# Moving the q and k transposes of an attention stage from TensorE to VectorE, with block-wise loads

## The chip, the core and the metric

The kernel runs on one core of one Trainium2 chip. The core has five instruction queues: TensorE (PE; its weight loads are listed as PEld), VectorE (DVE), ScalarE (ACT), GpSimd (POOL) and SyncE (SP), which here issues nearly all DMAs. They share SBUF; PE writes its results to PSUM. The metric is the device time of one execution in microseconds (us), lower is better.

## The reference, cut to what matters

A chain of three blocks: causal attention with a decay, then two MoE-like stacks of dense products. The change is in the attention.

```python
# q, k, v: (4, 8, 576, 64) float32;  f: (4, 8, 576)
scores = (1 / sqrt(64)) * q @ k.T
cum = cumsum(log(clip(f, 1e-4, 1)))
scores = where(causal, -1e9, scores + cum[:, None] - cum[None, :])
attn = exp(scores - max(scores)); attn = attn / (sum(attn) + 1e-9)
x = attn @ v            # heads side by side: (2304, 512)
h = (x @ w1) * (x @ w2) @ w3 @ w_out
h = h @ w_in            # 2048 wide
out = rational(h) @ w_out2
```

## The kernel before, in words

The order of all instructions is written out by hand; every engine runs its own queue in that order. The 32 heads are taken in 16 pairs, so that the two heads of 64 columns fill 128 partitions. A head has five steps (c = 0 to 4), one per chunk of 128 query rows (the last has 64), and step t = 5n + c of head n issues work of several heads: the scores of chunk c (`score_mm`, PE), their row-maximum (`score_max`, DVE, line 381), the exponential of the chunk before (`score_exp`, ACT, line 392), the normalisation of a group of chunks (`score_rcp` on DVE, `score_norm` on POOL, line 407), the transposes of the normalised probabilities of the next chunk in turn (`p_transpose`, PE, line 412) and their split in a high and a low part (`p_split`, ACT line 436 and DVE line 438; for heads below 8 a plain copy, lines 427 and 429). At the end of step 4 comes P x V of the head before (`pv`, PE into `ps_v`), for heads below 8 `pv_early` (PE into `ps_w`).

Every matrix product is done in three parts with operands split in a high and a low part. So q and k of a pair need d on the partitions, scaled and split. Before the change: `load_pair` (lines 286 to 292) brings rows of q or k into `q_raw` or `k_raw` with three DMAs, and `qk_transpose` (lines 301 to 304) transposes them on PE in five instructions into `v_ps`, 576 columns of the PSUM tile `ps_v` that `pv` also writes. `prep` (lines 306 to 315) then makes the high part on ACT (line 311, with the factor QKS = 1/8 for q) and the low part on DVE (line 313). `stack_q` and `stack_k` (lines 357 and 368) spread the parts over the operand tiles `qs`, `qb`, `kh`, `kc` with nine SBUF-to-SBUF DMAs, some of which wait for one another; `load_rows` (lines 330 and 331) adds the rows of `cum`. All these DMAs are issued by SP, in program order.

For pair p+1 this happens while pair p is worked on: at even n, q is transposed in step 1 (line 647) and prepared in step 2; k is transposed at the end of step 2 (line 715), after q's parts are read, and prepared in step 3. `load_rows` come in steps 0 and 1, the stack DMAs in steps 2 to 4. At odd n, the loads of pair p+2 are issued in steps 0 (q) and 1 (k), and those of v in step 4. The first pair is transposed ahead of the loop (lines 597 and 598), from other tiles for k.

Into these steps two further streams are woven: decoding of the weights (`HalfDecoder`: loads d_r on SP line 68, DVE lines 151 and 154, ACT, POOL), at steps listed in `DEC_AT` and later in steps 1 and 3; and, from head 9 on, filler matmuls: the products of the batch before with w1 and w2 (`gen_ab`, into the two banks `ps_f`, with a copy on ACT, line 550, and a product on DVE, line 553). `fill` issues them by a fixed credit per step. After the last head (about 370 us) come the remaining fillers and the dense stacks.

Of the kernel before, what the change touches and what calls it, by code (L numbers as in the profile page):

```python
# [19 lines left out]
P = 128  # L20
NCH = 5
# [12 lines left out]
def raw(ap):  # L34
    return ap.bitcast(F32)
# [138 lines left out]
def kernel(  # L174
# [78 lines left out]
    a_sb = [xp.tile([P, HB], F32, name=f"a_sb{i}") for i in range(2)]  # L253
    c_sb = [xp.tile([P, HB], F32, name=f"c_sb{i}") for i in range(3)]

    q_raw = ap_.tile([P, NCH, 2, D], F32, name="q_raw")
    k_raw = ap_.tile([P, NCH, 2, D], F32, name="k_raw")
    v_raw = ap_.tile([P, NCH, 2, D], F32, name="v_raw")
    vhl = [ap_.tile([P, NCH, 2, 2 * D], F32R, name=f"vhl{i}") for i in range(2)]

# [22 lines left out]
    def flat(t):  # L283
        return t.rearrange("p h d -> p (h d)")

    def load_pair(p, t, src):
        b, h0 = divmod(2 * p, H)
        for j in range(2):
            nc.sync.dma_start(
                t[:, 0:4, j], src[b, h0 + j, 0:512, :].rearrange("(c p) d -> p c d", p=P)  # L290
            )
        nc.sync.dma_start(t[0:64, 4], src[b, h0 : h0 + 2, 512:S, :].rearrange("h p d -> p h d"))
# [5 lines left out]
            out=t[:, :, :, D : 2 * D], in0=v_raw, in1=raw(t[:, :, :, 0:D]), op=ALU.subtract  # L298
        )

    def qk_transpose(t, ps, ps4):
        for c in range(4):
            nc.tensor.transpose(ps[:, P * c : P * (c + 1)], flat(t[:, c]), ident)  # L303
        nc.tensor.transpose(ps4, flat(t[0:64, 4]), ident[0:64, 0:64])

    def prep(p, w, step):
        i = p % 2
        h, l = (kh[i][0], klt) if w else (qs[i][0], qs[i][1])
        scale = 1.0 if w else QKS
        if step == 0:  # L310
            nc.scalar.mul(h, v_ps, scale)
        else:
            nc.vector.scalar_tensor_tensor(
                out=l, in0=v_ps, scalar=scale, in1=raw(h), op0=ALU.mult, op1=ALU.subtract
            )

    def rows_once(i):

# [13 lines left out]

    def first_q(j):
        r, o = HALF[j], HALF[1 - j]
        nc.scalar.mul(qs[0][j][r], v_ps[r], QKS)
        nc.vector.scalar_tensor_tensor(
            out=qs[0][j][o], in0=v_ps[r], scalar=QKS, in1=raw(qs[0][j][r]),
            op0=ALU.mult, op1=ALU.subtract,
        )
        nc.gpsimd.tensor_copy(qb[0][j][r], raw(qs[0][j][r]))  # L340

# [36 lines left out]
    def score_max(n, c, part):  # L378
        r, t = QN[c], NCH * n + c
        a, b = (0, min(EXT[c], 512)) if part == 0 else (512, EXT[c])  # L380
        nc.vector.tensor_tensor_reduce(  # L381
            out=pr[0:r, OFF[c] + a : OFF[c] + b],
            in0=ps_s[(t + part) % 2][0:r, 0 : b - a],
            in1=mask[0:r, 512 - Q0[c] + a : 512 - Q0[c] + b],
            scale=-1.0, scalar=3.0e38 if part == 0 else st4[0:r], op0=ALU.add, op1=ALU.min,
            accum_out=st4[0:r] if part == 0 and EXT[c] > 512 else st[0:r, 0, c : c + 1],
        )

# [183 lines left out]
    def fill(ns):  # L572
# [10 lines left out]
            credit[0] = 0.0  # L583

    nc.sync.dma_start(lf, f.rearrange("b h s -> (b h) s"))
    load_pair(0, q_raw, q)
    load_pair(0, k_raw, k)
    side.append(gen_w12())
    side_step()
    nc.gpsimd.memset(one, 1.0)  # L590
# [1 line left out]
    nc.vector.tensor_scalar(lf, lf, 1e-4, 1.0, op0=ALU.max, op1=ALU.min)  # L592
    nc.scalar.activation(lf, lf, AF.Ln)
    nc.vector.tensor_tensor_scan(cum, one, lf, 0.0, ALU.mult, ALU.add)
    nc.scalar.copy(crow[:, 0], cum)
    nc.vector.tensor_tensor(out=crow[:, 1], in0=cum, in1=raw(crow[:, 0]), op=ALU.subtract)
    qk_transpose(q_raw, v_ps, v_ps[:, 512:S])
    qk_transpose(k_raw, w_ps, w_ps[:, 512:S])
    first_q(0)
    first_k(0)  # L600
    load_pair(1, q_raw, q)
    load_rows(0, raw(crow[0:1]))
    load_rows(1, raw(crow[1:2]))
    load_pair(1, k_raw, k)
    nc.sync.dma_start(crow_dr, raw(crow))
    load_pair(0, vf[0], v)
    w12["dec"].ahead = 2
    nc.gpsimd.memset(mask, 0.0)
    nc.gpsimd.affine_select(
        mask[:, 512:], mask[:, 512:], pattern=[[-1, P]], compare_op=ALU.is_ge, fill=NEG, base=0,  # L610
        channel_multiplier=1,
    )
    nc.gpsimd.memset(st, 1.0)
# [10 lines left out]
    for t in range(NCH * (NH + 1) + 2):  # L624
        n, c = divmod(t, NCH)
        p, x = n // 2, t % 2
        live = n < NH
        m, cc = (n - 1, c + 1) if c < NCH - 1 else (n, 0)
        turn = 0 <= m < NH
        even = n % 2 == 0 and p + 1 < NPAIR  # L630
        if n < N32:
            grp = {3: (n, 0, 3), 0: (n - 1, 3, 5)}.get(c)
        else:
            grp = {2: (n, 0, 2), 4: (n, 2, 4), 0: (n - 1, 3 if n == N32 else 4, 5)}.get(c)
        if grp and not 0 <= grp[0] < NH:
            grp = None
        if turn:
            p_transpose(x, cc)
        if live and EXT[c] > 512:
            score_mm(n, c, 1)  # L640
        if live and c < NCH - 1:
            score_mm(n, c + 1, 0)
        if 0 <= n - 1 < N32:
            for qc in {2: (0, 1, 2), 3: (3,), 4: (4,)}.get(c, ()):
                pv_early(n - 1, qc)
        if even and c == 1:
            qk_transpose(q_raw, v_ps, v_ps[:, 512:S])
        if 0 < t <= NCH * NH:
            score_exp((c - 1) % NCH)
        if live:  # L650
            score_max(n, c, 0)
        if c == 1 and 0 <= n - 2 < N32:
            x_low(n - 2)
        if grp:
            score_rcp(grp[1], grp[2], 0)
        if late_x is not None:
            p_split(1 - x, *late_x, 1)
        if grp:
            score_rcp(grp[1], grp[2], 1)
        if live and EXT[c] > 512:  # L660
            score_max(n, c, 1)
        flush()
        if t == 10:
            w12["dec"].ahead = 4
        if t == T_X1:
            x_split(H + 1)
            side.append(gen_wo2())
            side_step()
            dec_due = False
        dec_now = t in DEC_AT or (t > T_X1 and c in (1, 3))  # L670
        if dec_now:
            side_step()
        if t == 0:
            first_q(1)
            first_k(1)
            rows_once(1)
            for tile_ in (v_raw, *vf):
                nc.gpsimd.memset(tile_[64:128, 4], 0.0)
            nc.gpsimd.memset(pr[0:64, OFF[4] + S : OFF[4] + 5 * P], 0.0)
            nc.sync.dma_start(pa_sb, pa.unsqueeze(0).to_broadcast([P, 4]))  # L680
            nc.sync.dma_start(pb_sb, pb.unsqueeze(0).to_broadcast([P, 2]))
        if even and c in (2, 3):
            prep(p + 1, c - 2, 0)
            prep(p + 1, c - 2, 1)
        if grp:
            for g in range(grp[1], grp[2]):
                score_norm(grp[0], g)
        if dec_due:
            side_step()
        dec_due = dec_now  # L690
        late_x = None
        if turn:
            p_split(x, m, cc, 0)
            late_x = (m, cc)
        if c == 0 and 0 <= n - 2 < NH:
            pv_out(n - 2)
        if c == 1 and n - 1 == N32:
            psw.close()
            psf = ps1.enter_context(
                tc.tile_pool(name="psf", bufs=1, space=PSUM, reuse_waits="tile")  # L700
            )
            ps_f += [psf.tile([P, 512], F32, name=f"ps_f{i}") for i in range(2)]
        if c == 1 and n % 2 == 1 and N32 <= n - 2 < NH and n not in (H + 3, H + 5, H + 7):
            x_split(n - 2)
        if n == H + 8 and c in (1, 3):
            x_split(H + 2 + c)
        if c == 4 and n % 2 == 0 and N32 <= n < NH:
            split_v(p)
        if c == 2 and n > H and n % H == 1 and n < NH:
            fillers.append(gen_ab(n // H - 1))  # L710
        if n == 4 and c == 2:
            nc.scalar.activation(pb_abs, pb_sb, AF.Abs)
        fill(FILL1[c])
        if even and c == 2:
            qk_transpose(k_raw, v_ps, v_ps[:, 512:S])
        if c == NCH - 1 and N32 <= n - 1 < NH:
            pv(n - 1)
        if c == NCH - 1 and n == N32:
            early.close()
            lp = late.enter_context(pool("late", "left"))  # L720
            pt += [lp.tile([P, NCH, PTS], F32R, name=f"pt{part}") for part in "hl"]
        if c == NCH - 1 and n + 1 < NH:
            score_mm(n + 1, 0, 0)
        if even and c < 2:
            load_rows(2 * (p + 1) + c)
        if even and c >= 2:
            stack_q(p + 1, c - 2)
        if even and c >= 3:
            stack_k(p + 1, c - 3)
        if n % 2 == 1 and p + 2 < NPAIR:  # L730
            if c == 0:
                load_pair(p + 2, q_raw, q)
            if c == 1:
                load_pair(p + 2, k_raw, k)
        if n % 2 == 1 and p + 1 < NPAIR:
            if c == 4:
                load_pair(p + 1, vf[(p + 1) % 2] if 2 * (p + 1) < N32 else v_raw, v)
# [333 lines left out]
```

## Time and profile before

| | |
|---|---|
| median of 3 runs | 1006.69 us (1006.63 to 1007.95) |
| the profiled execution: span from first to last instruction | 1007.3 us |
| busy time of DVE | 760.4 us (75%) |
| busy time of ACT | 658.0 us (65%) |
| busy time of POOL | 386.5 us (38%) |
| q1, the queue of all DMAs of SP: packets, share of 16 engines | 125808, 39.3% |

For the profiled execution no other time than its span is listed. Busy times of engines overlap and are averages over stages with different limits; a time in square brackets in a row is how long the engine stood idle before that instruction, and for what. Matmuls are pipelined, so the time from the start of one to the start of the next says more than the duration of one.

### The profile page before, as it was taken

What the parts mean: (1) busy time and instruction counts of PE and PEld (TensorE: products, weight loads), DVE (VectorE), ACT (ScalarE), POOL (GpSimd) and SP (SyncE); (2) the same over time, 40 slices, a digit from 0 to 9 for tenths busy, and PEclk for the clock granted to TensorE, in tenths of its full rate; (3) what the DMA queues carried; (4) which work ended last, traced back from release to release, by engine and by line L of the source; (5) the groups of instructions that cost most, each with busy time, mean ns of one, the idle gap of its engine ahead of it and who ended that gap; (6) DMA issues with size and microseconds to landing.
All of it is one profiled execution on the core that took longest, in us unless ns stands there. A gap on an engine that the chain in (4) does not pass through costs nothing.

```text
span 1007.3 us, 18126 instructions
## 1 busy us (share of the span) xinstructions
PE 978.1 (97%) x6032; PEld 859.5 (85%) x6032; DVE 760.4 (75%) x1690; ACT 658.0 (65%) x1443; POOL 386.5 (38%) x468
## 2 busy tenths in 40 slices
PE   6898999999999999999999999999999999999998
PEld 4676989999999999998899898888888888888886
DVE  5677886777777764979877729888788878877886
ACT  5677775766666663535555538767676767767686
POOL 7556772544444442644444302222222222222222
PEclk9999999999999999999999999999999999999999
DMA  5877664566666633664677651001001100100010
GB/s 130 216 179 199 187 141 116 145 186 182 175 175 183 165 103 111 199 211 160 201 246 242 211 159 37 1 14 70 1 1 42 43 1 8 37 20 1 1 43 21
DMA packets 125903, 114.94 MB, mean 114 GB/s; under 512 B 65521, under 2 KB 92145, under 8 KB 125809
## 3 DMA queue, kind: packets, MB, share of 16 engines
q1 hardware_dynamic: 125808, 113.79, 39.3%
q8 instruction: 47, 0.77, 0.3%
q14 instruction: 48, 0.39, 0.1%
HBM read 70.61 MB, written 23.22 MB: 93 GB/s over the span
## 4 chain that ended last, share of the span: by engine, by line
PE 79%; DVE 5%; DMA 3%; ACT 3%; issue 2%; SPq 1%; POOL 0%; ACTq 0%; DVEq 0%
PE bank L213 44%; PE ps_f L213 19%; PE ps_v L213 6%; PE ps_s L213 4%; PE ps_x L412 3%; PE ps_v L303 1%; DMA kh<-kh 1%; DMA wo2l<-wo_dr 1%; ACT rr L986 1%; DMA d_r<-in_moe_w_in_dram 1%; ACT rr L987 1%; DMA z_dr<-z_sb 1%; DVE pp L999 0%; DMA cl<-c_dr 0%; SPq L812 0%
## 5 line engine op out<-in xcount | busy, mean ns | idle before, releaser
L968 POOL TENSOR_TENSOR gl<-pp,gh 128x512 fp32r<-128x512 f32 (+1 forms) x80 | 95.3, 1191 | 318.5 <-ACT gh L967 312.0
L407 POOL TENSOR_SCALAR pr<-pr,st 128x128 f32<-128x128 f32 (+4 forms) x160 | 92.6, 590 | 145.2 <-DVE st L402 60.7
L381 DVE CUSTOM_DVE_ANT_0 pr<-ps_s,mask 128x128 f32<-128x128 f32 (+4 forms) x160 | 83.7, 523 | 71.4 <-PE ps_s L213 65.9
L213 PE MATMUL bank<-ch,wil 128*128 128x512 f32 (+1 forms) x320 | 118.3, 370 | 0.0
L213 PE MATMUL bank<-cl,wih 128*128 128x512 f32 (+1 forms) x320 | 118.2, 369 | 0.0
L213 PE MATMUL bank<-ch,wih 128*128 128x512 f32 (+1 forms) x320 | 117.8, 368 | 0.0
L213 PE MATMUL bank<-wo2h,gh 128*128 128x512 f32 x288 | 114.2, 397 | 0.8 <-ACT gh L967 0.8
L213 PE MATMUL bank<-wo2h,gl 128*128 128x512 f32 x288 | 114.1, 396 | 0.3
L213 PE MATMUL bank<-wo2l,gh 128*128 128x512 f32 x288 | 113.9, 396 | 0.0
L975 ACT ACTIVATE h<-bank 128x512 f32<-128x512 f32 (+1 forms) x80 | 44.3, 554 | 98.5 <-PE bank L213 98.4
L392 ACT ACTIVATE pr<-pr,st 128x128 f32<-128x128 f32 (+4 forms) x160 | 97.3, 608 | 12.7 <-DVE st L381 12.2
L982 DVE SCALAR_TENSOR_TENSOR qv<-h,pb_abs,qv 128x512 f32<-128x512 f32 (+1 forms) x80 | 55.8, 697 | 41.1 <-ACT qv L976 41.1
L436 ACT CAST pth<-ps_x 128x256 fp32r<-128x256 f32 (+1 forms) x96 | 44.5, 463 | 63.0 <-PE ps_x L412 43.5
L213 PE MATMUL bank<-cl,w3oh 128*128 128x256 f32 x288 | 81.4, 283 | 2.2 <-DVE cl L492 2.1
L213 PE MATMUL bank<-ch,w3oh 128*128 128x256 f32 x288 | 80.8, 280 | 1.1 <-ACT ch L491 1.0
L213 PE MATMUL bank<-ch,w3ol 128*128 128x256 f32 x288 | 80.6, 280 | 0.5 <-DVE w3ol L843 0.5
L412 PE MATMUL ps_x<-ident,pr 128*128 128x128 f32 (+1 forms) x480 | 74.7, 264 | 6.4 <-POOL pr L407 3.4
L213 PE MATMUL ps_s<-kh,qs 128*128 128x128 f32 (+2 forms) x192 | 75.6, 394 | 4.1 <-DMA kh<-kh 1.8
L992 DVE SCALAR_TENSOR_TENSOR qv<-qv,rr 128x512 f32<-128x512 f32 (+1 forms) x80 | 51.4, 643 | 28.5 <-ACT rr L987 28.5
L213 PEld LDWEIGHTS bank<-cl,wih 128*128 128x128 f32 x320 | 60.2, 188 | 11.7
L213 PEld LDWEIGHTS bank<-ch,wih 128*128 128x128 f32 x320 | 60.2, 188 | 11.7
L213 PEld LDWEIGHTS bank<-ch,wil 128*128 128x128 f32 x320 | 60.2, 188 | 10.3
(169 smaller groups left out, 3003.1 us busy)
## 6 DMA issues: line engine op xcount, KB each, us to landing
d_r<-in_moe_w_out_dram SPq DMA_DIRECT2D x48, 256.0 KB
c_dr<-c_sb SPq DMA_DIRECT2D x64, 144.0 KB
cl<-c_dr SPq DMA_DIRECT2D x36, 256.0 KB
d_r<-in_moe_w_dram SPq DMA_DIRECT2D x16, 512.0 KB
d_r<-in_moe_w_dram SPq DMA_DIRECT2D x32, 256.0 KB
d_r<-in_moe_w_in_dram SPq DMA_DIRECT2D x32, 256.0 KB
kh<-kh SPq DMA_DIRECT2D x45, 144.0 KB
z_dr<-z_sb SPq DMA_DIRECT2D x36, 128.0 KB
```

The costliest lines, as they stand in the source:

```text
L213: nc.tensor.matmul(o, lhsT, rhs, start=start, stop=stop)
L303: nc.tensor.transpose(ps[:, P * c : P * (c + 1)], flat(t[:, c]), ident)
L381: nc.vector.tensor_tensor_reduce(out=pr[0:r, OFF[c] + a : OFF[c] + b], in0=ps_s[(t + part) % 2][0:r, 0 : b - a], in1=mask[0:r, 512 - Q0[c] ...
L392: nc.scalar.activation(x, x, AF.Exp, bias=st[0:r, 0, c : c + 1], scale=-1.0, accum_out=st[0:r, 1, c : c + 1],)
L407: nc.gpsimd.tensor_scalar(x, x, st[0:r, 1, c : c + 1], 1.0, op0=ALU.mult, op1=ALU.mult)
L412: nc.tensor.transpose(ps_x[x][:, r * j : r * (j + 1)], pr[0:r, o + P * j : o + P * (j + 1)], ident[0:r, 0:r],)
L436: nc.scalar.copy(hi, src)
L968: nc.gpsimd.tensor_tensor(out=at(gl, j), in0=at(pp, j), in1=raw(at(gh, j)), op=ALU.subtract)
L975: nc.scalar.activation(at(h2, i), h, AF.Square)
L982: nc.vector.scalar_tensor_tensor(out=at(qv, i), in0=at(h2, i), scalar=pb_abs[:, 1:2], in1=at(qv, i), op0=ALU.mult, op1=ALU.add,)
L986: nc.scalar.activation(at(rr, i), at(qv, i), AF.Ln, bias=ln_bias, scale=2.0**-62)
L992: nc.vector.scalar_tensor_tensor(out=at(qv, i), in0=at(qv, i), scalar=QC, in1=at(rr, i), op0=ALU.add, op1=ALU.mult)
```

## The change

From pair 1 on, q and k are no longer loaded as rows. `load_blocks` loads them as blocks of 32 x 32: on partition 64j + 32g + p stands, for each of 18 groups n of rows, row 32n + p of head j, columns 32g to 32g + 31. A DVE transpose, which works on each block of 32 x 32 by itself, then puts d on the partitions, in one instruction of 128x576, into the same PSUM place that PE's transposes wrote. q's DVE transpose stands in step 1 of an even head, k's in step 2 behind q's parts. A pair's loads are eight DMAs instead of six, and are issued two per step over steps 0 to 3 of an odd head. The factor 1/8 is taken from q's parts and put in the row-maximum; the `cum` rows and the mask's fill are multiplied by 8 to make up for it. The first pair is still loaded as rows and transposed on PE.

```diff
-    q_raw = ap_.tile([P, NCH, 2, D], F32, name="q_raw")
-    k_raw = ap_.tile([P, NCH, 2, D], F32, name="k_raw")
+    raws = [ap_.tile([P, NCH * 2 * D], F32, name=nm) for nm in ("q_raw", "k_raw")]
+    q_raw, k_raw = (t[:, 0:S] for t in raws)
+    q_rows, k_rows = (t.rearrange("p (c j d) -> p c j d", c=NCH, j=2) for t in raws)
...
+    def load_blocks(p, t, src, heads=range(2)):
+        b, h0 = divmod(2 * p, H)
+        for j in heads:
+            for g in range(2):
+                o, d = 64 * j + 32 * g, slice(32 * g, 32 * (g + 1))
+                nc.sync.dma_start(
+                    t[o : o + 32].rearrange("p (n d) -> p n d", d=32),
+                    src[b, h0 + j].rearrange("(n p) d -> p n d", p=32)[:, :, d],
+                )
...
-    def prep(p, w, step):
+    def prep_t(w):
+        nc.vector.transpose(v_ps, k_raw if w else q_raw)
+
+    def prep_hl(p, w):
         i = p % 2
         h, l = (kh[i][0], klt) if w else (qs[i][0], qs[i][1])
-        scale = 1.0 if w else QKS
-        if step == 0:
-            nc.scalar.mul(h, v_ps, scale)
-        else:
-            nc.vector.scalar_tensor_tensor(
-                out=l, in0=v_ps, scalar=scale, in1=raw(h), op0=ALU.mult, op1=ALU.subtract
-            )
+        nc.scalar.copy(h, v_ps)
+        nc.vector.tensor_tensor(out=l, in0=v_ps, in1=raw(h), op=ALU.subtract)
...
-            scale=-1.0, scalar=3.0e38 if part == 0 else st4[0:r], op0=ALU.add, op1=ALU.min,
+            scale=-QKS, scalar=3.0e38 if part == 0 else st4[0:r], op0=ALU.add, op1=ALU.min,
...
-    nc.scalar.copy(crow[:, 0], cum)
-    nc.vector.tensor_tensor(out=crow[:, 1], in0=cum, in1=raw(crow[:, 0]), op=ALU.subtract)
-    qk_transpose(q_raw, v_ps, v_ps[:, 512:S])
-    qk_transpose(k_raw, w_ps, w_ps[:, 512:S])
+    nc.scalar.mul(crow[:, 0], cum, 1.0 / QKS)
+    nc.vector.scalar_tensor_tensor(
+        out=crow[:, 1], in0=cum, scalar=1.0 / QKS, in1=raw(crow[:, 0]),
+        op0=ALU.mult, op1=ALU.subtract,
+    )
+    qk_transpose(q_rows, v_ps, v_ps[:, 512:S])
+    qk_transpose(k_rows, w_ps, w_ps[:, 512:S])
...
-    load_pair(1, q_raw, q)
+    load_blocks(1, q_raw, q)
     load_rows(0, raw(crow[0:1]))
     load_rows(1, raw(crow[1:2]))
-    load_pair(1, k_raw, k)
+    load_blocks(1, k_raw, k)
...
-        if even and c == 1:
-            qk_transpose(q_raw, v_ps, v_ps[:, 512:S])
...
+        if even and c == 1:
+            prep_t(0)
         if even and c in (2, 3):
-            prep(p + 1, c - 2, 0)
-            prep(p + 1, c - 2, 1)
+            prep_hl(p + 1, c - 2)
+        if even and c == 2:
+            prep_t(1)
...
-        if even and c == 2:
-            qk_transpose(k_raw, v_ps, v_ps[:, 512:S])
...
-        if n % 2 == 1 and p + 2 < NPAIR:
-            if c == 0:
-                load_pair(p + 2, q_raw, q)
-            if c == 1:
-                load_pair(p + 2, k_raw, k)
+        if n % 2 == 1 and p + 2 < NPAIR and c < 4:
+            load_blocks(p + 2, (q_raw, k_raw)[c // 2], (q, k)[c // 2], (c % 2,))
```

## Rows read from the trace of the kernel before

**Rows 1.** The page, busy time, share of the span and instructions of PE:

```profile
PE 978.1 (97%) x6032; PEld 859.5 (85%) x6032; DVE 760.4 (75%) x1690; ACT 658.0 (65%) x1443; POOL 386.5 (38%) x468
```

**Rows 2.** The page, shares of the chain that ended last, by engine:

```profile
PE 79%; DVE 5%; DMA 3%; ACT 3%; issue 2%; SPq 1%; POOL 0%; ACTq 0%; DVEq 0%
```

**Rows 3.** Windows: length, then busy us of each engine, PE clock, DMA share, GB/s:

```profile
60.00:80.00 20.00, 17.93 (x135) 13.41 (x133) 15.30 (x50) 15.98 (x44) 12.31 (x17) 1.00 0.74 196
...
120.00:145.00 25.00, 23.37 (x173) 21.80 (x172) 21.45 (x56) 18.59 (x47) 20.12 (x21) 1.00 0.56 135
145.00:170.00 25.00, 25.00 (x189) 23.67 (x187) 14.93 (x54) 15.06 (x39) 9.52 (x14) 1.00 0.51 127
...
295.00:320.00 25.00, 25.00 (x188) 23.68 (x187) 18.28 (x66) 16.76 (x46) 11.81 (x17) 1.00 0.70 188
```

**Rows 4.** Chain in order of time (start, us, what): P x V, one per head:

```profile
155.21 1.70 PE ps_v L213 x12
...
168.28 1.71 PE ps_v L213 x12
...
353.80 1.70 PE ps_v L213 x12
...
365.53 1.71 PE ps_v L213 x12
```

**Rows 5.** Timeline of PE in heads 12 and 26 (start, us, instruction):

```profile
144.28 0.92 PE L213 MATMUL ps_v<-ptl,vhl 128*128 128x448 f32 x5
...
308.38 0.60 PE L303 MATMUL ps_v<-ident,q_raw 128*128 128x128 f32 x4
...
309.12 0.40 PE L213 MATMUL ps_f<-xl,w2h 128*128 128x288 f32 x1
...
317.93 0.92 PE L213 MATMUL ps_v<-ptl,vhl 128*128 128x448 f32 x5
```

**Rows 6.** Timeline of DVE in heads 10 (end), 12 and 26:

```profile
118.81 0.29 DVE L381 CUSTOM_DVE_ANT_0 pr<-ps_s,mask 128x128 f32<-128x128 f32 x1 [0.23 <-PE ps_s L213]
...
143.28 0.49 DVE L438 TENSOR_TENSOR ptl<-ps_x,pth 128x320 fp32r<-128x320 f32 x1
...
310.89 0.46 DVE L553 TENSOR_TENSOR c_sb<-ps_f,a_sb 128x288 f32<-128x288 f32 x1 [0.27 <-PE ps_f L213]
...
314.69 0.76 DVE L313 SCALAR_TENSOR_TENSOR klt<-ps_v,kh 128x576 fp32r<-128x576 f32 x1 [0.70 <-ACT kh L311]
...
316.04 0.48 DVE L438 TENSOR_TENSOR ptl<-ps_x,pth 128x320 fp32r<-128x320 f32 x1
```

**Rows 7.** Groups of DVE by line and shape, to 650 us: busy, mean ns | idle before:

```profile
L468 DVE TENSOR_TENSOR xr<-ps_v,xtmp 64x576 f32<-64x576 f32 x24 | 18.1, 755 | 10.3 <-ACT xtmp L467 10.3
...
L313 DVE SCALAR_TENSOR_TENSOR klt<-ps_v,kh 128x576 fp32r<-128x576 f32 x15 | 11.3, 755 | 10.2 <-ACT kh L311 9.5 <-DMA qb<-crow_dr 0.7
...
L427 DVE COPY ptf<-ps_x 128x320 f32<-128x320 f32 x8 | 3.8, 474 | 1.5 <-PE ps_x L412 1.5
```

**Rows 8.** Waits of PE and DVE up to 375 us: total us, times, longest:

```profile
PE ps_v L303 <- DVE qs L313: 3.0, 3, 1.6
...
PE ps_s L213 <- DMA kh<-kh: 1.8, 3, 1.1
...
DVE klt L313 <- ACT kh L311: 9.5, 12, 1.4
```

**Rows 9.** Timeline of SP: first and last of a pair's q and k loads:

```profile
65.53 1.14 SPq L289 DMA_DIRECT2D q_raw<-in_q_dram  x2
...
68.66 0.65 SPq L292 DMA_DIRECT2D k_raw<-in_k_dram  x1
```

**Rows 10.** DMA packets and queue q1 in the first 3.6 us:

```profile
DMA packets 1047, 0.32 MB, mean 90 GB/s; under 512 B 1015, under 2 KB 1015, under 8 KB 1047
...
q1 hardware_dynamic: 1046, 0.32, 37.8%
```

More of the change, by code (lines that the diff above doesn't have):

```diff
@@ L284, in flat, with qk_transpose @@
         return t.rearrange("p h d -> p (h d)")
+    def qk_transpose(t, ps, ps4):
+        for c in range(4):
+            nc.tensor.transpose(ps[:, P * c : P * (c + 1)], flat(t[:, c]), ident)
+        nc.tensor.transpose(ps4, flat(t[0:64, 4]), ident[0:64, 0:64])
+    def load_blocks(p, t, src, heads=range(2)):
[7 more added lines that the diff above has]
+                )
     def load_pair(p, t, src):
@@ L299, in split_v @@
         )
[L301 to L304, printed above, removed]
-    def prep(p, w, step):
+    def prep_t(w):
+        nc.vector.transpose(v_ps, k_raw if w else q_raw)
+    def prep_hl(p, w):
         i = p % 2
         h, l = (kh[i][0], klt) if w else (qs[i][0], qs[i][1])
-        scale = 1.0 if w else QKS
-        if step == 0:
-            nc.scalar.mul(h, v_ps, scale)
-        else:
-            nc.vector.scalar_tensor_tensor(
-                out=l, in0=v_ps, scalar=scale, in1=raw(h), op0=ALU.mult, op1=ALU.subtract
-            )
+        nc.scalar.copy(h, v_ps)
+        nc.vector.tensor_tensor(out=l, in0=v_ps, in1=raw(h), op=ALU.subtract)
     def rows_once(i):
@@ L334, in first_q @@
         r, o = HALF[j], HALF[1 - j]
[L335 to L338, printed above, removed]
+        nc.scalar.copy(qs[0][j][r], v_ps[r])
+        nc.vector.tensor_tensor(
+            out=qs[0][j][o], in0=v_ps[r], in1=raw(qs[0][j][r]), op=ALU.subtract
         )
@@ L585 @@
     nc.sync.dma_start(lf, f.rearrange("b h s -> (b h) s"))
-    load_pair(0, q_raw, q)
-    load_pair(0, k_raw, k)
+    load_pair(0, q_rows, q)
+    load_pair(0, k_rows, k)
     side.append(gen_w12())
@@ L609 @@
     nc.gpsimd.affine_select(
-        mask[:, 512:], mask[:, 512:], pattern=[[-1, P]], compare_op=ALU.is_ge, fill=NEG, base=0,
+        mask[:, 512:], mask[:, 512:], pattern=[[-1, P]], compare_op=ALU.is_ge, fill=NEG / QKS, base=0,
         channel_multiplier=1,
```

## The prediction, made before the changed kernel ran

> **What bounds the kernel now.** I read the page from the top. TensorE (PE) is busy nearly all the span [rows 1], and the chain that ended last lies on it for about four fifths [rows 2]; a busy share is an average, so I next read the stages. The change lies only in the attention part, up to about 370 us. Its windows [rows 3] fall into three kinds. In the first batch (heads 0 to 7, no filler matmuls) PE has gaps, VectorE (DVE) works 15.3 us of 20 and the DMA engines 74%. Around heads 10 to 12 the last decoding of w1 and w2 still runs beside filler matmuls: DVE 21.5 us of 25, PE 23.4. From head 13 on PE has no gap at all, while DVE has a third to a quarter of its time free. Here, where PE sets the pace, the removed transposes are worth something.
>
> What they are worth is read from the chain in time order, at the starts of the P x V matmuls, one per head [rows 4]. Head 14, an even one with transposes, takes 168.28 - 155.21 = 13.07 us. Head 30, even but without transposes since no pair follows, takes 365.53 - 353.80 = 11.73. So one pair's transposes cost 1.34 us of PE pace. The timeline agrees: from the first q transpose of head 26 to the next filler 309.12 - 308.38 = 0.74 us [rows 5], and k's set is alike. Eight such heads (14, 16, ... 28) lie in the PE-bound stretch: 10.7 us is the ceiling there.
>
> **Part 1, transposes from PE to DVE.** Fifteen pairs lose ten PE transposes each and gain two DVE transposes of 128x576. No row shows a DVE transpose. The nearest of the full size are DVE's passes over 576 columns, 755 ns whether with a scalar or as a plain tensor-tensor [rows 7]; as both forms cost the same, the new plain subtract is costed at nothing, as are ScalarE's copy for its multiply and the other constant in the row-maximum, which keep instruction and size. The lower end is the one-source copy of 320 columns, 474 ns; the upper is two passes, 1510 ns, as an element is four bytes. I take 755, the row of the same size: 1.51 us per even head. [...]
>
> Does DVE have the room? What counts is when it delivers the last low part of the transposed probabilities, which P x V reads. In head 26 that instruction ends at 316.04 + 0.48 = 316.52 [rows 6], and PE starts on it at 317.93 [rows 5]: slack 1.41. After the change PE would be there 1.34 earlier, at 316.59. DVE is later by 1.51, less the idle 0.27 and 0.70 in this head [rows 6] (it waited there for a filler and for ScalarE's k copy, and will not as it is late itself): 316.52 + 1.51 - 0.97 = 317.06. So PE waits 0.47 and the head gains 1.34 - 0.47 = 0.87. Heads 16 to 28, seven of this pattern: -6.1 us. Head 14 has no decoding (DVE 14.9 us of 25 [rows 3]) and keeps its 1.34: together -7.4.
>
> Head 12 decodes twice and has no idle time to give: 143.28 + 0.49 + 1.51 = 145.28 against 144.28 - 1.34 = 142.94 [rows 5, 6], a stall of 2.34, so +1.0 net. In head 10 DVE ends only 0.23 before it gets the next head's scores [rows 6] and is itself the path: 1.51 - 0.23 = +1.3. In heads 0 to 8 I count nothing for DVE: behind k's transposes sits the same chain (ScalarE's k copy, DVE's k low part); DVE waited 9.5 us over 12 times for that copy, and PE 3.0 us for q's low part to free the PSUM tile [rows 8]. DVE's own transpose (0.75) follows its subtract at once instead of PE's set, which is as long. If this cover fails, each of the four heads 2 to 8 costs up to 0.75, +3.
>
> What is queued behind the new instructions: on DVE the row maximum of step 2 stands behind q's transpose and that of step 3 behind k's. Both find scores already written, and ScalarE's exponentials come a step later. q's copy on ScalarE now waits for DVE, not PE; ScalarE is less than 70% busy here, so no wait is added on the path.
>
> **Part 2, the loads.** SP issues all of them in order. Before, a pair's q and k are six DMAs, from 65.53 to 68.66 + 0.65 = 69.31: 3.78 us [rows 9]. Now they are eight. A block DMA is not in the trace; its ends are 0.28 us (half of a present one, as it moves half the bytes) and 0.65 (the dearest here), and I take 0.57, half of the 1.14 for two, whose shape is nearest: 8 x 0.57 with seven gaps of 0.05 is 4.9, +1.1 us per pair of SP time. The ends give -1.2 and +1.8. From head 13 on SP has pauses and the tiles come a head early: nothing. In the first batch it isn't free: SP goes straight from the last stack DMA of one pair through loads of q, k, weights and v to the row loads and stack DMAs of the next, and PE then waits for the last of these, kh, three times, 1.8 us in all [rows 8]. That ring binds the starts of heads 4, 6 and 8: 3 x 1.1 = +3.3, with ends of -3.6 and +5.4. The first pair keeps its loads; one DMA more ahead of the first row loads (0.57) stands against PE's wait for q's low part in head 0, and I set both to nothing.
>
> The bytes stay, the packets halve from 256 to 128 B: 2304 per pair become 4608. In the first 3.6 us, when the queue moved hardly anything but 256 B packets, 1046 took 37.8% of 16 engines [rows 10]: 0.378 x 16 x 3600 / 1046 = 20.8 ns each. A half-sized one costs between 10.4 and 20.8 ns, so a pair's load of 3.0 us of all engines becomes 3.0 to 6.0. From head 13 on, at 51 to 70% and 25 us a pair [rows 3], even 3 us more leave room. In the first batch, at 74%, it may not: a rival below; between ends far apart I take the lower, as the SP issue there is as slow as the engines. [...]
>
> **Sum.** -7.4 + 1.0 + 1.3 + 3.3 = -1.8 us on the profiled execution (span 1007.3, which is 0.6 above the median of the runs), so on the median 1006.69 - 1.8 = 1004.9. With DVE at 474 ns no stall is left in heads 16 to 28: 8 x -1.34 + 0.4 + 0.7 + 3.3 = -6.3. With DVE at 755 and the loads no dearer than now it is -5.1; with the loads at their upper end, +0.3. Stage 3 and everything after 370 us hold PE nearly without gaps, so what is gained or lost reaches the end.
>
> **Rivals.**
> - *DVE has room and the loads are hidden*: 474 ns each, and SP no dearer. For it: its free quarter from head 13 on, and its 2 to 3 us of waiting at each head's start. Against it: the slack of 1.41 before P x V is what counts. Time: 8 x -1.34 + 0.4 + 0.7 = -9.6, so 997.1.
> - *The transposes make DVE the bound (slower).* Place: DVE before P x V in even heads. Price: two passes, 1.51 us each, 1.51 more per even head than I take. It decides from about 0.95 us each on, where the sum passes +2. At 1.51 heads 16 to 28 give 7 x (1.51 - 0.87) = +4.5, head 14 still -1.3, heads 12 and 10 +2.5 and +2.8, heads 2 to 8 +3, loads +3.3: +14.8, so 1021.5. For it: nothing on DVE writes PSUM today. Against it: all full passes over 576 columns cost 755.
> - *The small packets bind the first batch (slower).* A packet of 128 B costs what one of 256 B does: 3 us more engine time for each of three pairs, +9 in place of 3.3: sum +3.9, so 1010.6. For it: 74% busy. Against it: SP's pauses around the stack DMAs.
> - *It does not do what it says*: the compiler cuts the DVE transpose at the PSUM bank edge, or a wait on the shared tile keeps PE where it was. Then about nothing changes.
>
> **How the numbers follow.** A measurement of this kernel can tell about 0.2%, 2 us, from no change. My own case gets 0.55, spread from -6 to +3; its middle lies at the edge of 2 us, and more of its costs are bounds than prices, so half of it is faster, 0.28, within 0.22, slower 0.05. Full room: 0.16, all faster. DVE the bound: 0.12 slower. Packets: 0.12, of which 0.02 within. Not as said: 0.05, within. That makes faster 0.44, within 0.29, slower 0.27. The range from 998 to 1011 leaves out the slow-transpose case and the far end of the full-room one. The likeliest case's own range is 1001 to 1010.
>
> **What would show it.** Right: PE's transposes of q_raw and k_raw gone but for pair 0's ten; thirty DVE transposes of 128x576 near 755 ns; even heads from 16 on near 12.2 us, with PE waiting some 0.5 us for DVE's low part before P x V; heads 10 and 12 longer; the first batch's pairs about a microsecond longer with PE waiting for kh. Wrong: a DVE transpose beyond 1 us, even heads at 11.7 or above 13.1, DVE waiting for q_raw or k_raw from DMA, or block DMAs beyond 0.65 us on SP.

## The result, and the profile after

The changed kernel takes 1017.0 us (median of 4 runs, 1015.99 to 1017.78) against 1007.32 of the kernel before on the same chip (1006.63 to 1010.14): ratio 1.0082, 95% interval 1.0060 to 1.0104. I forecast 1004.9 in 998 to 1011, with faster as the likeliest sign. It is slower, and outside the range.

The page of the changed kernel, the lines that answer to [rows 1, 2], with the granted clock by slices of 25 us between them:

```profile
PE 965.6 (95%) x5882; PEld 849.5 (84%) x5882; DVE 777.0 (77%) x1720; ACT 659.3 (65%) x1443; POOL 386.2 (38%) x468
...
PEclk9989799999999999999999999999999999999999
...
PE 74%; DMA 8%; DVE 7%; SPq 3%; ACT 3%; issue 3%; POOL 1%; POOLq 0%; DVEq 0%; ACTq 0%
```

The change did what it says: PE has 150 instructions fewer and is busy 12.5 us less, DVE has 30 more. Yet PE's share of the chain fell from 79 to 74%, and DMA and SP's queue gained seven points together. TensorE's clock, 1.00 in every window of before that I read, now dips in the first slices.

Where the time went is read from a few starts. Two timelines of PE, each with the first score matmuls of heads 4, 8 and 10 and the P x V matmuls of heads 13 and 28; first the kernel before:

```profile
49.85 0.30 PE L213 MATMUL ps_s<-kh,qs 128*128 128x128 f32 x1 [1.09 <-DMA kh<-kh]
...
85.04 0.30 PE L213 MATMUL ps_s<-kh,qs 128*128 128x128 f32 x1 [0.34 <-DMA kh<-kh]
...
105.18 0.30 PE L213 MATMUL ps_s<-kh,qs 128*128 128x128 f32 x1
...
155.04 0.22 PE L213 MATMUL ps_v<-pt0h,vhl 128*128 128x128 f32 x1
...
341.92 0.23 PE L213 MATMUL ps_v<-pt0h,vhl 128*128 128x128 f32 x1
```

The same five of the changed kernel:

```profile
51.64 0.30 PE L213 MATMUL ps_s<-kh,qs 128*128 128x128 f32 x1 [0.96 <-issue]
...
95.78 0.30 PE L213 MATMUL ps_s<-kh,qs 128*128 128x128 f32 x1 [0.76 <-DMA kh<-kh]
...
121.30 0.30 PE L213 MATMUL ps_s<-kh,qs 128*128 128x128 f32 x1
...
173.53 0.22 PE L213 MATMUL ps_v<-pt0h,vhl 128*128 128x128 f32 x1
...
351.29 0.33 PE L213 MATMUL ps_v<-pt0h,vhl 128*128 128x128 f32 x1
```

| stretch | before | after | difference | forecast |
|---|---|---|---|---|
| to the scores of head 4 | 49.85 | 51.64 | +1.8 | |
| heads 4 to 7 | 35.19 | 44.14 | +8.95 | |
| heads 8 and 9 | 20.14 | 25.52 | +5.4 | all three: +3.3 |
| heads 10 to 13 | 49.86 | 52.23 | +2.4 | +2.3 |
| heads 14 to 28 | 186.88 | 177.76 | -9.1 | -7.4 |

(The fourth row runs from the scores of head 10 to P x V of head 13.) What follows head 28 holds the same instructions before and after and took 665.4 and 663.3 us. Over all profiled runs of this study it lies between 660.8 and 666.5, so this -2.1, which makes the sum up to the +7.3 of the spans, tells nothing of the change. The gain came, in the heads where PE sets the pace, and a bit more of it than forecast. The whole miss lies in the first batch: +16.1 by head 9, where I had +3.3.

Four windows of the changed kernel (length, busy us of each engine, PE's granted clock, DMA share, GB/s), the last two as in [rows 3]:

```profile
62.00:68.00 6.00, 4.99 (x26) 4.36 (x27) 4.50 (x18) 3.97 (x11) 4.99 (x7) 0.50 0.42 102
...
106.00:116.00 10.00, 8.54 (x39) 7.45 (x38) 7.58 (x27) 6.76 (x18) 5.47 (x7) 0.50 0.85 202
...
145.00:170.00 25.00, 23.33 (x169) 21.93 (x170) 20.38 (x65) 17.55 (x44) 16.44 (x19) 1.00 0.54 122
295.00:320.00 25.00, 25.00 (x185) 23.73 (x184) 20.33 (x67) 18.18 (x49) 12.28 (x17) 1.00 0.77 191
```

In the first batch PE ran some microseconds at a granted clock of 0.50 in four stretches, each time after it had stood idle for 2.6 to 4.6 us. Not every such wait did it: after 2.86 us at 144 us the clock stayed at 1.00, as the third window shows. In 295 to 320 it has no gap, as before, and DVE has taken the work over, 20.3 us for 18.3.

What made PE idle stands in the chain in order of time (start, us, what), here from the stack DMA of pair 2 to the normalisation that waits in the end:

```profile
44.20 4.90 DMA kh<-kh
...
53.21 0.39 SPq L68
53.64 6.62 DMA k_raw<-in_k_dram
...
60.29 0.42 DMA qb<-crow_dr
...
60.74 0.06 DVE ps_v L318
...
62.59 0.38 POOL pr L415
63.01 0.48 PE ps_x L420
```

One of the last k blocks takes 6.62 us from issue to landing; DVE's transpose of k waits for it (and 0.4 us more for one small DMA), the row-maximum behind it in DVE's queue waits too, then the normalisation on POOL and PE's transposes of the probabilities. The same wait for k comes again 23 us later, in head 6, and a third time in head 8, where PE waits for the row-maximum itself. SP's queue in that stretch shows what stands ahead of those blocks:

```profile
52.01 1.04 SPq L297 DMA_DIRECT2D k_raw<-in_k_dram  x2
53.21 0.39 SPq L68 DMA_DIRECT2D d_r<-in_moe_w_dram  x1
53.64 1.01 SPq L297 DMA_DIRECT2D k_raw<-in_k_dram  x2
...
55.83 3.29 SPq L308 DMA_DIRECT2D vf<-in_v_dram  x1
```

L68 is a load of 512 KB of weights. It goes out in step 3, between the k blocks of step 2 and those of step 3, so only the second half of k stands behind it. Before, k's loads went out in step 1, ahead of it. And the waits up to 375 us (total us, times, longest), where the kernel before waits for k once, for 0.8 us, ahead of the loop:

```profile
PE ps_x L420 <- POOL pr L415: 16.2, 10, 4.6
...
DVE ps_v L318 <- DMA k_raw<-in_k_dram: 5.3, 2, 2.7
```

The wait of the chain above, 3.57 us on DVE, isn't among these 5.3: it is put down to the small DMA that landed last.

### The profile page after: what moved, and what is told of

It reads as the page before. It is cut to its first block, busy times and chain, and to the rows that moved or that the text cites. A ratio compares the mean times of both kernels' runs of the same rounds, so it can differ in the third digit from the quotient of the medians.

```text
span 1014.6 us, 17892 instructions
## 1 busy us (share of the span) xinstructions
PE 965.6 (95%) x5882; PEld 849.5 (84%) x5882; DVE 777.0 (77%) x1720; ACT 659.3 (65%) x1443; POOL 386.2 (38%) x468
## 4 chain that ended last, share of the span: by engine, by line
PE 74%; DMA 8%; DVE 7%; SPq 3%; ACT 3%; issue 3%; POOL 1%; POOLq 0%; DVEq 0%; ACTq 0%
PE bank L213 40%; PE ps_f L213 19%; PE ps_v L213 6%; PE ps_s L213 4%; PE ps_x L420 4%; DMA k_raw<-in_k_dram 2%; DMA z_dr<-z_sb 2%; DMA kh<-kh 2%; SPq L297 1%; DMA cl<-c_dr 1%; DVE cl L500 1%; DVE pr L389 1%; SPq L819 1%; ACT rr L993 1%; ACT rr L994 1%
## 5 line engine op out<-in xcount | busy, mean ns | idle before, releaser
L420 PE MATMUL ps_x<-ident,pr 128*128 128x128 f32 (+1 forms) x480 | 78.7, 274 | 22.8 <-POOL pr L415 16.2
L213 PE MATMUL ps_s<-kh,qs 128*128 128x128 f32 (+2 forms) x192 | 78.1, 407 | 7.9 <-DVE st L389 4.3
L420 PEld LDWEIGHTS ps_x<-ident,pr 128*128 128x128 f32 (+1 forms) x480 | 52.8, 145 | 34.7 <-POOL pr L415 22.6
L999 DVE SCALAR_TENSOR_TENSOR qv<-qv,rr 128x512 f32<-128x512 f32 (+1 forms) x80 | 51.6, 645 | 28.5 <-ACT rr L994 28.5
```

What stands on the lines that cost most here:

```text
L213: nc.tensor.matmul(o, lhsT, rhs, start=start, stop=stop)
L420: nc.tensor.transpose(ps_x[x][:, r * j : r * (j + 1)], pr[0:r, o + P * j : o + P * (j + 1)], ident[0:r, 0:r],)
L999: nc.vector.scalar_tensor_tensor(out=at(qv, i), in0=at(qv, i), scalar=QC, in1=at(rr, i), op0=ALU.add, op1=ALU.mult)
```

## The experiments

From the trace three causes offered themselves for the first batch: **A**, the order of the loads (k later, behind the weights); **B**, the block loads themselves (more DMAs on SP, twice the packets); **C**, DVE's transposes, which I had counted at nothing there. Each experiment is read twice: by the time, and by the length of heads 4 to 7 (first scores of head 4 to first scores of head 8), which is the cleanest measure of the first batch. Two kernels that do there exactly or in kind what the kernel before does (e4, e6) took 35.4 and 35.1 us. But e11, which has the same instructions in these heads, took 37.9 in its profiled run (PE waits 1.7 us for kh after head 5, and head 6 has a clock of 0.83). So the length of one run can be 2.7 us off, as much as some of the terms below, and under e4 they are set against the times of all runs. Single starts are no better: head 2 alone took 10.1 us in the profiled run of before and 12.9 in e6, whose PE had a clock of 0.87 from 28.5 to 41.8 us.

**e1: only the order put back.** Blocks and DVE transposes stay; q's blocks go out in step 0, k's in step 1.

```diff
-        if n % 2 == 1 and p + 2 < NPAIR and c < 4:
-            load_blocks(p + 2, (q_raw, k_raw)[c // 2], (q, k)[c // 2], (c % 2,))
+        if n % 2 == 1 and p + 2 < NPAIR and c < 2:
+            load_blocks(p + 2, (q_raw, k_raw)[c], (q, k)[c])
```

> The block loads of a pair go back to where the row loads stood: all four of q in step 0 of an odd head, all four of k in step 1. Theory A (order): in the changed kernel the second half of k's blocks is issued behind a 512 KB weight load, lands some 6 us later, and DVE, which has to transpose k in its turn, waits for it in heads 2 to 8; then most of the 16 us that the P x V of head 9 is late by goes, it starts below 110 us (103.6 before the change, 119.8 after), and the time is 1003 to 1008 us. Theory B (load): the two more DMAs on SP and the doubled packets themselves cost it, wherever they are issued; then the P x V of head 9 stays near 119 and the time at 1014 to 1018. Theory C (DVE): DVE's two transposes are what the first batch cannot carry; same numbers as B.

Measured: 1010.86 us, ratio to before 1.0009 (0.9990 to 1.0029). Heads 4 to 7 take 40.23 us in place of 44.14. So the order costs some 2.0 us a pair, and is the largest single cause; but 5 us are left. A had hoped for more: 1003 to 1008 us, and P x V of head 9 below 110 us, where it starts at 111.24. The order of e1 also isn't free later on: heads 14 to 28 take 180.52 us in place of 177.76.

**e2: rows again, DVE transposes kept.** The loads are those of before; the transposed tiles then hold other values than q and k of the reference, on the same shapes.

```diff
...
-            load_blocks(p + 2, (q_raw, k_raw)[c // 2], (q, k)[c // 2], (c % 2,))
+            load_pair(p + 2, (q_rows, k_rows)[c], (q, k)[c])
```

> Loads as before the change (six DMAs of rows per pair, in steps 0 and 1), transposes on DVE as in the changed kernel; since rows are then transposed block by block, the scores are those of other operands, so the output means nothing, but every instruction has its size. Theories A and B: the first batch is as before or at most 3 us longer, heads 14 to 28 take 11.7 to 11.95 us each, the time is 996 to 1001. Theory C: the first batch stays 10 us or more behind, 1010 or more.

Measured: 1005.26 us, ratio 0.9948 (0.9930 to 0.9967), between the two forecasts. Timeline of PE, the first scores of heads 4 and 8, and a window:

```profile
51.02 0.30 PE L213 MATMUL ps_s<-kh,qs 128*128 128x128 f32 x1 [1.66 <-DMA kh<-kh]
...
88.86 0.30 PE L213 MATMUL ps_s<-kh,qs 128*128 128x128 f32 x1 [1.01 <-DMA kh<-kh]
```

```profile
98.00:106.00 8.00, 7.18 (x31) 5.97 (x29) 6.19 (x22) 5.97 (x15) 5.34 (x7) 0.57 0.85 230
```

Heads 4 to 7 take 37.84 us, +2.65 over before with the loads untouched: if it is not scatter, DVE's transposes cost 1.3 us a pair in the first batch, all of it in heads 5 and 7. Head 9 (12.67 us, before 10.77) adds 1.9, with the clock at 0.57 in that stretch. Against e1, with the same order and transposes, the blocks cost 40.23 - 37.84 = 2.4, or 1.2 a pair; a part of that may be the clock, which was 1.00 in e2 from 50 to 96 us and 0.93 in e1.

**e3: blocks spread over steps 0 to 3 as in the change, PE's transposes.** (The transposed values again differ.)

```diff
+        if even and c == 1:
+            qk_transpose(q_rows, v_ps, v_ps[:, 512:S])
...
-        if even and c == 1:
-            prep_t(0)
...
-        if even and c == 2:
-            prep_t(1)
...
+        if even and c == 2:
+            qk_transpose(k_rows, v_ps, v_ps[:, 512:S])
```

> Loads by blocks as in the changed kernel, transposes on PE as before (they then transpose blocks, so the output means nothing). Theory A: k is as late as in the changed kernel and PE waits in DVE's place; the P x V of head 9 at 113 to 121 us, even heads from 14 on at 13.1 again, the time 1018 to 1028. Theory B: the same, or somewhat less if only SP's time counts: 1011 to 1015. Theory C: the first batch is as before, 1006 to 1010.

Measured: 1019.59 us, ratio 1.0092 (1.0073 to 1.0112); heads 4 to 7 take 39.92 us. The loads alone cost 4.7 there, without any work moved to DVE (a part of it may be the clock, 0.93 from 50 to 96 us), and the gain of the later heads is missing, since PE still transposes.

**e5: the kernel before, its row loads spread over steps 0 to 3.** `load_half` issues the rows of one head; the one DMA for the last 64 rows of both goes with the second.

```diff
...
-        if n % 2 == 1 and p + 2 < NPAIR:
-            if c == 0:
-                load_pair(p + 2, q_raw, q)
-            if c == 1:
-                load_pair(p + 2, k_raw, k)
+        if n % 2 == 1 and p + 2 < NPAIR and c < 4:
+            load_half(p + 2, (q_raw, k_raw)[c // 2], (q, k)[c // 2], c % 2)
```

> The kernel before the change with one thing altered: a pair's row loads are spread over the steps 0 to 3 of the odd head (q of the first head, q of the second with the rest of both, the same for k), still six DMAs of 256 B packets, transposes on PE. Theory A: k's second half stands behind the weight load here too and PE's transpose of k waits: 3 to 12 us slower than before. Theories B and C: within 0.2% of the kernel before.

Measured: 1011.63 us, ratio 1.0018 (0.9999 to 1.0037); heads 4 to 7 take 36.61 us, +1.4. That is below the 3 to 12 us that A gave and, with a clock of 0.96 from 50 to 96 us, not clear of the scatter, though PE's transposes of k wait for its rows here too (0.80 us at 75.48 us and 1.43 at 93.86). The later place costs rows less than blocks. The terms do not simply add: spread blocks (+4.7) and DVE (+2.65) make 7.4, the change has 8.95. On DVE a wait for k also stops the row-maxima behind it (3.57 us in the chain of the change); that this is why the terms grow together is argued, not tested.

**e9: as the change, k's blocks put ahead of the weights.** The blocks of k stay in steps 2 and 3 but go out at the head of the step, those of step 3 so ahead of the weight load of step 3 (the expectation says step 2).

```diff
+        if n % 2 == 1 and p + 2 < NPAIR and c in (2, 3):
+            load_blocks(p + 2, k_raw, k, (c - 2,))
         if dec_now:
             side_step()
...
```

> The changed kernel with k's block loads of steps 2 and 3 put at the head of the step, ahead of the weight load of step 2 in SyncE's queue. Theory O1 (k waits behind the 512 KB weight load's packets): most of the loss of order goes, head 9's P x V product starts at 110 to 114 us in place of 119.6, and the time is 1009 to 1012 us. Theory O2 (k is late because it is issued two steps later, whatever lies ahead of it): head 9 starts at 117 to 120 us and the time stays 1015 to 1018 us.

Measured: 1009.32 us, ratio 1.0007 (0.9987 to 1.0026). SP's queue at the same place as above:

```profile
49.67 2.27 SPq L297 DMA_DIRECT2D q_raw<-in_q_dram  x4
51.99 2.12 SPq L297 DMA_DIRECT2D k_raw<-in_k_dram  x4
54.27 0.38 SPq L68 DMA_DIRECT2D d_r<-in_moe_w_dram  x1
...
57.39 0.66 SPq L308 DMA_DIRECT2D vf<-in_v_dram  x1
```

Timeline of PE, first scores of heads 4 and 8:

```profile
51.67 0.30 PE L213 MATMUL ps_s<-kh,qs 128*128 128x128 f32 x1 [0.47 <-issue]
...
91.36 0.30 PE L213 MATMUL ps_s<-kh,qs 128*128 128x128 f32 x1 [0.88 <-DMA kh<-kh]
```

The chain in order of time, at the landing of k in the same pair:

```profile
53.61 4.22 DMA k_raw<-in_k_dram
```

This is the cleanest of the set. The last k block is issued by 54.11 us, in the change by 54.65: half a microsecond apart. Only what stands ahead of it differs. From issue to landing k takes 4.22 us in place of 6.62, DVE's transpose of k starts at 57.95 in place of 60.74, and heads 4 to 7 fall from 44.14 to 39.69, P x V of head 9 from 119.6 to 111.55 us, as O1 said. It isn't the later step that costs, it is the 512 KB in front. That k's packets themselves wait behind those of the weights is my reading of the two landings, 6.62 us behind them and 4.22 ahead of them; the order in which the DMA engines take packets was not shown.

**e7: the kernel before with DVE transposes that nobody reads.** PE still does the real ones; in heads 0, 2, 4 and 6 DVE makes one more pass for q and for k at the places of the change.

```diff
...
+        if even and c == 1 and n < N32:
+            nc.vector.transpose(spare, flat_q)
...
+        if even and c == 2 and n < N32:
+            nc.vector.transpose(spare, flat_k)
```

> The kernel before with one VectorE transpose of 128x576 more for q and one for k in heads 0, 2, 4 and 6, at the places that the change uses, into a buffer that nobody reads; TensorE still makes the real transposes. Theory D (VectorE's time is in series with the first batch's chain): of the 8 x 0.79 = 6.3 us added, more than half shows: the scores of head 8 start 3 to 6 us after the 85.0 us of before, and the time is 1010 to 1013 us. Theory P (VectorE had room, and what costs in the changed kernel is that TensorE, with less to do, is granted the lower clock): TensorE keeps its work here, the granted clock stays at 1.00 in 40 to 100 us, head 8 starts within 1.5 us of before, and the time is that of before within 2 us.

Measured: 1014.74 us, ratio 1.0056 (1.0035 to 1.0076). Timeline of PE, first scores of heads 4 and 8, and a window:

```profile
53.83 0.30 PE L213 MATMUL ps_s<-kh,qs 128*128 128x128 f32 x1 [1.97 <-DMA kh<-kh]
...
91.15 0.30 PE L213 MATMUL ps_s<-kh,qs 128*128 128x128 f32 x1 [0.69 <-DMA kh<-kh]
```

```profile
40.00:110.00 70.00, 59.21 (x456) 46.44 (x455) 53.03 (x168) 51.46 (x135) 42.71 (x55) 1.00 0.74 187
```

Head 8 starts 6.1 us late, but 3.8 of that arose in head 0, where the first added pass waited 3.3 us for POOL to clear the tile that it writes: a fault of the experiment, so its time is no measure. Heads 4 to 7 are free of it: 37.32 us, +2.1, or 1.1 a pair out of the 1.53 added (0.77 us each here), with all of PE's work in place and the clock at 1.00 from 40 to 110. As in e2 the excess lies in heads 5 and 7. The clock, at 1.00, can't be what costs here, so P doesn't explain them; D, that DVE's time is in series with the first batch's chain, does. It is likely and not shown: e11 is longer in the same two heads (9.65 and 8.92 us, before 8.34 and 8.32) without such passes, and by the time some 1.9 of the ratio's 5.6 us are left beside head 0, no more than the noise.

**e6: the scale alone moved.** q is split unscaled, the decay rows and the mask are multiplied by 8, the row-maximum multiplies by 1/8.

```diff
...
-            scale=-1.0, scalar=3.0e38 if part == 0 else st4[0:r], op0=ALU.add, op1=ALU.min,
+            scale=-QKS, scalar=3.0e38 if part == 0 else st4[0:r], op0=ALU.add, op1=ALU.min,
...
```

> The kernel before with only the scale moved: q is copied and split unscaled, the decay rows and the mask are divided by it, and the row maximum multiplies by it. The number of instructions on each engine and their shapes stay; the time is that of before within 0.2% (every theory). If VectorE's split or the row maximum took longer in the new form, the DVE rows would show it and the time would rise by more than 2 us.

Measured: 1009.89 us, ratio 0.9999 (0.9979 to 1.0020). Nothing, as expected; the scale has no part in what follows.

**e4: the change from pair 8 on only.** Pairs 0 to 7 keep rows and PE's transposes.

```diff
...
+    PBLK = 8
...
+        if even and c == 1 and p + 1 < PBLK:
+            qk_transpose(q_rows, v_ps, v_ps[:, 512:S])
...
-        if even and c == 1:
+        if even and c == 1 and p + 1 >= PBLK:
             prep_t(0)
...
```

> Pairs 0 to 7 as in the kernel before (rows, TensorE's transposes), pairs 8 to 15 as in the changed one (blocks, VectorE's transposes). If the changed kernel's loss lies in the first batch alone and its gain in the heads bound by TensorE alone, the P x V product of head 9 starts within 2 us of the 103.5 us of before, each of heads 14 to 28 takes 11.7 to 11.95 us in place of 13.0, and the time is 996 to 1000 us. If instead the block loads or VectorE's extra work cost something there too that the late start had hidden, the heads take 12.4 us or more and the time is 1003 us or above.

Measured: 1001.69 us (999.89 to 1003.01), ratio 0.9922 (0.9895 to 0.9949): it beats both kernels. Timeline of PE, P x V of heads 13 and 28:

```profile
157.89 0.22 PE L213 MATMUL ps_v<-pt0h,vhl 128*128 128x128 f32 x1
...
335.63 0.33 PE L213 MATMUL ps_v<-pt0h,vhl 128*128 128x128 f32 x1
```

177.74 us for heads 14 to 28 against 186.88 before: -9.1, the same as in the change. The ratio makes it a gain of 7.9 us, a little less than forecast; the profiled run reaches head 9 at 106.3, 2.8 us later than that of before, because of its head 2 (13.0 us, with the clock at 0.86 in 30 to 40 us), which is the spread spoken of above.

e4 has the later heads of the change, so what another kernel with these later heads takes beyond it is the price of its first pairs, by all runs and each against the kernel before on its own chip: the change 16.1 us (1.0082 less 0.9922), e1 8.8, e9 8.6, e2 2.6. The intervals of the change and of e9 do not meet, nor do those of e1 and e2; those of e2 and e4 do. So the order (7.6 us, the change less e9) and the blocks (6.2 us, e1 less e2, of which 2.8 lie in heads 14 to 28 in the profiled runs) are clear of noise. DVE's passes in the first batch are not: their cost rests on the profiled runs of e2 and e7.

**e10 and e11: filler for the clock.** Here theory C is another one, that part of the loss is the lower clock after PE's long waits; N says that it is not. Both kernels add transposes of the identity into a part of `ps_v` that isn't read; e10 to the change, e11 to e4.

```diff
+        if even and c == 4 and 2 <= n <= N32:
+            for _ in range(20):
+                nc.tensor.transpose(ps_v[:, 0:P], ident, ident)
         if turn:
             p_transpose(x, cc)
```

> The changed kernel with 20 more TensorE transposes of the identity into an unread part of ps_v in step 4 of heads 2, 4, 6 and 8, where TensorE waits 2.6 to 4.6 us for late k. They take about 20 x 0.16 = 3.3 us at full clock, inside that wait. Theory C (part of the loss is the lower granted clock after these waits, 0.50 in 62 to 68, 86 to 88 and 106 to 116 us): the granted clock stays nearer 1.00 in 40 to 120 us, heads 5, 7 and 9 take 8.4, 8.4 and 11.0 us in place of 9.2, 9.4 and 13.1, head 9's P x V product starts 3 to 5 us earlier than 119.6, and the time is 1012 to 1014 us. Theory N (the late transfers and VectorE set these heads, whatever the clock): head 9 stays at 119 to 121 us and the time at 1016 to 1018 us.

Measured: 1018.32 us, ratio 1.0095 (1.0070 to 1.0120). Timeline of PE: the first filler of head 6, then the first scores of heads 9 and 10; and the window of heads 8 and 9:

```profile
86.36 0.33 PE L650 MATMUL ps_v<-ident 128*128 128x128 f32 x1 [3.00 <-DVE klt L324]
...
111.78 0.33 PE L213 MATMUL ps_s<-kh,qs 128*128 128x128 f32 x1
...
122.58 0.30 PE L213 MATMUL ps_s<-kh,qs 128*128 128x128 f32 x1
```

```profile
98.90:122.60 23.70, 18.96 (x147) 16.21 (x145) 16.46 (x52) 15.71 (x41) 15.53 (x18) 1.00 0.78 171
```

The fillers write the tile that k's low part is read from and so waited for it; they came after the idle time, not in it, and their own 2.4 to 4.5 us a time went on the path. By the time, N. By head 9, C: with the clock at 1.00 it takes 10.80 us, in the change 13.09 with the clock at 0.70, before 10.77. e1, whose work in that head is the change's, takes 10.75 at 1.00 too. So the clock is worth 2.3 us in head 9, which the fillers cost again. Head 7 (7.77 us, in the change 9.41 at 0.88, before 8.32) decides nothing: e1 and e2 take 9.75 and 9.80 there at 1.00.

e11 has 14 such fillers in step 2 of head 2.

> The hybrid (rows and TensorE's transposes up to pair 7, blocks and VectorE's from pair 8) with 14 more TensorE transposes of the identity in step 2 of head 2, where TensorE waited 3.0 us for VectorE's split of q and the granted clock fell afterwards (0.86 in 30 to 40 us). Theory C: the clock stays at 1.00 in 30 to 50 us, head 2 takes 10 to 11.5 us in place of 13.0, and the time falls by 1 to 2.5 us from the hybrid's 1001.7 us. Theory N: head 2 stays at 12.5 to 13.5 us, and the time is the hybrid's within 0.5 us, or longer by what of the fillers isn't hidden.

Measured: 1004.13 us, ratio 0.9947 (0.9931 to 0.9964). By the ratios it is 2.5 us slower than e4, and the fillers themselves take 2.6; the first of them in the timeline of PE:

```profile
36.94 0.33 PE L731 MATMUL ps_v<-ident 128*128 128x128 f32 x1 [3.10 <-DVE qs L324]
```

Again they stood behind the wait that they were to fill: the clock is 0.88 from 30 to 40 us, and head 2 takes 14.76 us. In the profiled run the fillers aren't the loss, though. The scores of head 4 start at 51.61 us, in e4 at 51.70; the loss comes in heads 4 to 7, 37.91 us in place of 35.44 with the same instructions. Why the runs of e11 are slower stays open. A filler into a tile of its own wasn't tried; what the clock costs in the first batch as a whole stays open.

## Why the prediction was wrong

**The heads bound by PE: right, a little small.** I forecast -7.4 for heads 14 to 28 and it was -9.1, in e4 too: the even heads gain 10.0 of the ceiling of 10.7, and the odd ones lose 0.9. The DVE transposes are two groups of the right kind and nearly the size taken (785 and 794 ns for 755):

```profile
L318 DVE STREAM_TRANSPOSE ps_v<-k_raw 128x576 f32<-128x576 f32 x15 | 11.9, 794 | 10.1 <-DMA k_raw<-in_k_dram 5.3 <-DMA qb<-crow_dr 3.6 <-DMA vf<-in_v_dram 0.8
L318 DVE STREAM_TRANSPOSE ps_v<-q_raw 128x576 f32<-128x576 f32 x15 | 11.8, 785 | 0.3 <-DMA q_raw<-in_q_dram 0.2
```

The term that was mis-sized is PE's stall before P x V, 0.47 us a head. Head 26 in the timeline:

```profile
327.86 0.48 DVE L446 TENSOR_TENSOR ptl<-ps_x,pth 128x320 fp32r<-128x320 f32 x1
328.23 0.30 PE L213 MATMUL ps_v<-pt0l,vhl 128*128 128x128 f32 x1
...
328.39 0.97 PE L213 MATMUL ps_v<-ptl,vhl 128*128 128x448 f32 x5
```

DVE's last low part ends at 328.34, and PE reads it at 328.39 without a gap: DVE comes just in time, where I had it 0.47 late. Head 26 takes 11.84 us, not 12.2. I had moved PE 1.34 us forward and left DVE's start where it was; but a PE that is ahead also gives DVE its scores earlier. That last sentence is argued, not tested.

**Heads 10 to 13: the sum by luck.** Forecast +1.0 for head 12 and +1.3 for head 10, measured +2.4 for the four. By the starts of P x V, though, head 10 has +0.4, head 12 +0.3 and head 11 +1.7. Over all runs these have two sources. The 0.3 to 0.4 come with DVE's transposes: e2 has them and takes 13.40 us in head 10, e3 hasn't and takes 13.07, as before. Head 11 goes with the block loads: it takes 15.3 to 17.3 us in the five kernels with block loads there, e3 with PE's transposes among them, and 13.6 to 13.9 in the seven with row loads, e2 among them. What waits there wasn't tried. I had these heads at +2.3 for DVE and nothing for the loads.

**"In heads 0 to 8 I count nothing for DVE": likely wrong.** Two profiled runs speak against it. In them the cover that I named, ScalarE's k copy, hid little of it: two DVE passes of 0.77 to 0.79 us a pair cost 1.1 (e7) to 1.3 us (e2) of pace. By that my bound for a cover that fails, 0.75 a head, was too low as well, since it held one transpose of the two. By the times of all runs, 2.6 us for e2 beyond e4, the cost isn't clear of noise.

**The loads: the issue right, the order missing.** This is the step that failed. I priced part 2 as SP's issue, 4.9 us a pair in place of 3.78; SP's queue shows 49.69 to 54.65, or 4.96, and blocks against rows in the same order cost 1.2 us a pair (e1 against e2) where I had 1.1. That fit is in part luck: e1's clock was lower in these heads (0.93 for 1.00), and by all runs the blocks cost 6.2 us where I had 3.3. But the change also moves k's loads from step 1 to steps 2 and 3, and half of them so past the weight load of step 3. I looked at how long SP is busy and not at what it issues ahead of k, 512 KB of weights. e9 and e1 put that at 2 us a pair in heads 4 to 7, and at 8 of the 16 us by head 9; by all runs it is 7.6 us. The sign that I had named for being wrong, DVE waiting for k_raw from DMA, is there. Beside it the clock, which I had taken as given at the 1.00 of [rows 3], added in heads behind long waits: 2.3 us in head 9, as e10 and e1 show.

**The packets: the lower end.** A window of the changed kernel's DMA view, in which all but eight packets are under 512 B, 132 B in the mean:

```profile
DMA packets 2806, 0.37 MB, mean 136 GB/s; under 512 B 2798, under 2 KB 2798, under 8 KB 2806
...
q1 hardware_dynamic: 2806, 0.37, 82.7%
```

0.827 x 16 x 2700 ns / 2806 = 12.7 ns a packet, nearer to the 10.4 that I took than to 20.8.

**The rivals.** None happened. The packets were to bring the sum to +3.9 and the transposes to +14.8; the loss, in the largest part, came from a wait that none of my cases held, a load issued behind a larger one (72 KB behind 512). I should have asked of the moved loads what each queue holds ahead of them.

## What to carry to other kernels

A DMA that is moved in the program order of its issuing engine can land later because of what it now stands behind (6.62 us in place of 4.22 here): before pricing its issue, list that, in bytes. Price work put on an engine stage by stage: the same transposes won 9 us where TensorE sets the pace, and won nothing in the first batch, where the chain ran through VectorE's queue behind a late load. A change whose gain and loss lie in different stages can be applied by stage, as e4 does.

## What the runs showed of the hardware

- In the change TensorE's clock fell to 0.50 after waits of 2.6, 4.6, 3.6 and 2.8 us. Head 9 takes 10.75 to 10.80 us in nine kernels, with a clock of 1.00 in every window read there, and 12.3 to 13.1 in the three others (0.70 in the change, 0.57 in e2 from 98 to 106 us, 0.83 in e9 from 100 to 110), so a late transfer was paid for twice there. But a wait alone doesn't settle it: in e7 the clock stayed at 1.00 after one of 4.0 us in head 0, and in e2 it fell at 98 us with no wait longer than 1.01 us in the 13 us before.
- SP's issue is no fixed price: the last vf DMA of pair 2 held SP for 3.29 us in the change and for 0.66 in e9, with the same DMAs in another order. In part the time only moved: the two vf DMAs ahead of it took 0.99 and 2.54, so the three together 4.28 and 3.20, and 2.83 before. Why wasn't tried.
- The stage after head 28 has the same instructions in every kernel and took between 660.8 and 666.5 us. Single profiled executions are compared by stage, not by their spans.
